# A gated linear attention fused with a cosine-gated MLP: products handed to VectorE in the first five pairs, a fourth load buffer, DMA turns one pair earlier, and a new order of steps

## The chip, the core and the metric

The kernel runs on one core of a Trainium2 chip. Its time is device microseconds of one execution, and the number compared is the median of several executions. Three executions of the kernel before took 182.08, 183.91 and 185.15 us, so the median is 183.91 us and the spread is about 1.7%.

## What is computed

Attention with a forget gate runs over 4 batches and 8 heads, 768 positions of 48 values each. Its output is laid out as 3072 rows of 384 values and goes through two matrices with `h * cos(h)` between them.

```python
f = 1.0 / (1.0 + np.exp(-f_logit))
for t in range(S):
    state = f[:, :, t, :, None] * state + np.einsum('bhd,bhe->bhde', k[:, :, t], v[:, :, t])
    y[:, :, t] = np.einsum('bhd,bhde->bhe', q[:, :, t], state)
h = x @ w_in           # x: 3072 x 384, w_in: 384 x 2048
g = h * np.cos(h)
out = g @ w_out        # w_out: 2048 x 384
```

Inputs and output are float32. Inside the kernel the matrix products run in bfloat16.

## The kernel before

**Tiling.** The 768 positions of a batch are cut into stretches of 256, which the code calls pairs (two chunks of 128, or two positions to each of 128 partitions). There are 12 pairs, three to a batch, and the state of a batch runs through its three pairs. The MLP works on units of tokens: units 0 and 1 are the two halves of pair 0 (128 rows each), and unit m from 2 on is pair m-1 (256 rows).

**Steps of a pair n.** Every step has a name, and the names are used below.

- Loads `f n`, `k n`, `q n`, `v n` bring 384 KB each from device memory (line 296). Pairs 0 and 1 load f, k and q in two halves of four heads, `f0.0` and `f0.1` and so on.
- ScalarE makes the gate: `ex` (exp, L329), `ln` (L333), `fx` (exp again, L347), `fy` (add one, L344).
- `qa` (L338 or L341) multiplies q by a gate, `ka` (L351) multiplies k by a gate, and `ad` (L363) adds two logarithms. `cum` (L374 and L380, TensorE) sums the logarithms over time, and `eb` and `ei` (L391 or L395, ScalarE) take the exponential of the sums.
- `qm` and `km` (L404) multiply q and k by these exponentials and write the tile `qk` in bfloat16. They come in two halves of four heads.
- Turning: in pairs 0 to 4 `tq` and `tk` transpose `qk` on TensorE (L434, sixteen 128x128 transposes a pair), and `qkt` copies the result out of PSUM (L439; the profile shows the copies at their helper's line L197). In pairs 5 to 11 two DMA transposes do it (L423), issued by the SP queue.
- `vb` casts v and `vt` (four of them) places it with zeroes around it (L197).
- `sc` makes the scores (L454, TensorE) and `am` masks them (L458, VectorE). `ps` is the outer product for the state (L476); `st` (L494) and `sz` (L500) carry and decay the state on VectorE. `y` and `yi` (both L528) sum the output, and `xe` copies it to SBUF.

**Steps of a unit m.** `h` is the first product (L576), twelve matmuls of 128 columns or six of 256 for each step; `co` is the cosine on ScalarE (L581); `g` multiplies h by it on VectorE (L558); `o` is the second product (L592, four matmuls of 384 columns each); `ot` copies a row block out, and `out` stores it (L603). The weights come in eight pieces: `w0.x` is a piece of w_in, `w1.x` one of w_out, 768 KB each (L282), cast by `wc` (L197).

**PSUM and fillers.** PSUM has eight banks. `h`, `co`, `g`, `sc` and `am` use two banks at a time, so four such values can be in flight, and an `h` step waits for the `g` or `am` that last used its banks. `zf` steps (L264) are matmuls of zeroes, 51 of them, that stand between TensorE's first real steps.

**Order.** No planner runs when the kernel is built. The string `ORDER` (L36 to L117) lists all steps in one sequence, each with its engine (T TensorE, S ScalarE, V VectorE, G GpSimd, Y SP) and the buffer or bank that its result takes. `emit` (L617) writes them out in that sequence, and each engine then does its own steps strictly in order. A step that may run on more than one engine names them in `G.step(...)`, and the letter in `ORDER` picks one. `SLOTS` (L30) is the number of buffers of each kind. The loads run on the queues of SP and ScalarE, and a load waits for the load eight places ahead of it in the program, besides the users of its buffer.

In the profile VectorE is DVE and GpSimd is POOL.

Of the kernel before, what the change touches and what calls it, by code (L numbers as in the profile page):

```python
# [15 lines left out]
B, H, S, D = 4, 8, 768, 48  # L16
# [20 lines left out]
f0.0:Y0 f0.1:Y zf0:T0 zf1:T2 q0.0:Y2 zf2:T3 zqk.2:G zf3:T4 k0.0:Y1 zf4:T5 zf5:T6 f1.0:Y2 zf6:T7  # L37
zf7:T1 k0.1:Y zf8:T0 zf9:T2 v0:Y1 zf10:T3 zsz.0:V zf11:T4 zsp.0:V f1.1:Y zsz.3:V ex0.0:S zf12:T5
zvt.0:V zf13:T6 zvt.1:V zf14:T7 ln0.0:S0 k1.0:Y2 zf15:T0 fx0.0:S cum0.0:T1 ex0.1:S f3:Y1 zf16:T2
zf17:T3 zf18:T4 ln0.1:S zf19:T5 k1.1:Y ka0.0:V zf20:T6 fx0.1:S cum0.1:T7 q0.1:S zf21:T0 q1.0:Y1  # L40
zf22:T2 zf23:T3 eb0.0:S0 zf24:T4 ei0.0:S1 zf25:T5 v1:Y0 ei0.1:S zf26:T6 km0.0:V2 eb0.1:S zf27:T1
ex1.0:S ka0.1:V zf28:T0 zf29:T7 zvt.2:V zf30:T2 qa0.0:V ln1.0:S0 zf31:T3 q1.1:Y qm0.0:V vb0:G2
fx1.0:S cum1.0:T6 zsp.1:V tk0.0:T0 km0.1:V tq0.0:T ex1.1:S vt0.2:G1 ps0.0:T3,2 ps0.1:T zf32:T4
ln1.1:S zqk.1:G sz0.01:V0 zf33:T5 ei1.0:S2 cum1.1:T7 vt0.0:G eb1.0:S2 qa0.1:V tk0.1:T4 qkt0.0:S3
sz0.00:V zf34:T6 f2:Y0 qm0.1:G zf35:T1 st0.11:V zf36:T3 w0.0:Y1 zf37:T5 sz0.11:V3 fx1.1:S w0.1:Y4
sc0.0:T0 ka1.0:G ei1.1:S st0.10:V tq0.1:T eb1.1:S zf38:T6 sz0.10:V ex3:S zf39:T7 km1.0:G0 qkt0.1:V0
zf40:T3 zf41:T2 am0.0:V2 ln3:S1 yi0:T5 sc0.1:T2 vt0.1:G zf42:T4 zf43:T6 fx3:S ad3:G0 zf44:T7 qa1.0:V
zf45:T4 vt0.3:S zf46:T0 qm1.0:V zf47:T1 zqk.0:V vb1:G1 cum3:T6 ka1.1:V tk1.0:T7 am0.1:V0 eb3:S1
tq1.0:T km1.1:G ps1.0:T0,1 qkt1.0:S3 zf48:T4 zf49:T4 zf50:T4 qa1.1:V ps1.1:T vt1.1:G2 vt1.3:S
sc1.0:T2 zsp.2:V qm1.1:V y0:T7 ex2:S st1.00:V q3:Y1 tq1.1:T4 am1.0:V0 tk1.1:T w0.2:Y3 ei3:S0 ln2:S0  # L50
qkt1.1:V4 wc0.0:G vt1.2:S sz1.00:V0 xe0.1:S0 st1.01:V xe0.0:S sz1.01:V sc1.1:T4 ad2:G2 w0.3:Y1
vt1.0:S yi1:T0,3 am1.1:V2 fx2:S k3:Y2 h0.00:T6 fy3:S w1.0:Y2 wc0.1:G cum2:T2 y1:T ei2:S1 xe1.0:S1
h1.00:T4 xe1.1:V qa3:G eb2:S0 h1.01:T st1.11:V st1.10:V qm3.1:G2 h2.00:T2 sz1.11:V3 sz1.10:V h0.01:T
co1.0:S2 qm3.0:G h2.01:T co0.0:S0 wc0.2:G q2:Y1 g1.0:V4 h2.11:T0 h2.10:T co2.0:S1 g0.0:V0 wc0.3:G
h2.20:T4 co2.1:S2 h2.21:T g2.0:V3 h1.10:T6 ka3:G w1.1:Y1 co2.2:S3 f5:Y2 h1.11:T g2.1:V km3.0:G fy2:S
h0.10:T2 k2:S0 h0.11:T wc1.0:G g2.2:V co1.1:S0 h2.31:T0 co0.1:S1 g1.1:V h2.30:T qa2:G w1.2:Y2
o0.0:T5 v2:Y0 co2.3:S3 zsz.2:V qm2.1:G1 g0.1:V o1.0:T6 o2.0:T4 qm2.0:G wc1.1:S g2.3:V tq3.1:T7
tq3.0:T2 tk3.0:T km3.1:G tq2.0:T3 o0.1:T qkt3.0:V0 w1.3:Y1 ka2:G v3:Y2 o2.1:T f4:Y1 k5:Y1 tk3.1:T
ex5:S km2.0:G sc3.0:T0 q4:Y2 qkt3.1:V4 o1.1:T ln5:S0 am3.0:V2 km2.1:G tk2.0:T tq2.1:T2 o3.1:T7 fx5:S
ad5:G0 qkt2.0:V2 f7:Y0 wc1.2:S tk2.1:T o3.0:T qkt2.1:V3 sc2.0:T0 sc3.1:T2 fy5:S vb2:G0 am2.0:V3  # L60
# [128 lines left out]
def describe(nc, cpool, ppool, q, k, v, f_logit, moe_w_in, moe_w_out, out):  # L189
# [121 lines left out]
    def pair(n):  # L311
# [38 lines left out]
        def lead_k(e, t, w):  # L350
            eng(e).tensor_mul(out=w.ap[:, :, 0, :], in0=w.ap[:, :, 0, :], in1=t.ap[:, :, 0, :])  # L351
# [363 lines left out]
```

## Time and profile before

| what | us |
|---|---|
| median of three executions (182.08 to 185.15) | 183.91 |
| the execution that was profiled | 182.69 |
| its span, first to last instruction | 180.9 |
| TensorE busy | 171.6 (95%) |
| VectorE busy | 140.1 (77%) |
| ScalarE busy | 128.4 (71%) |
| GpSimd busy | 108.8 (60%) |

The profile is of one execution, and times in it run from its first instruction. The execution took 1.8 us more than its span. A busy share is an average over stages: VectorE, ScalarE and GpSimd are all busy for nine tenths of some stretches in the first 100 us, and GpSimd has nothing left after about 131 us. TensorE's busy time holds 49 recorded filler matmuls. Matmuls overlap, so the time from one start to the next is a better price than a duration.

### The profile page before, as it was taken

To read this page: it belongs to the slowest core of one execution; us is meant where nothing else is said; L and a number is where in the kernel's file an instruction comes from. 1 tells how busy PE (TensorE), PEld (TensorE's weight loads), DVE (VectorE), ACT (ScalarE), POOL (GpSimd) and SP (SyncE) were. 2 spreads that over 40 slices of the span, in tenths; PEclk is the share of its full clock that TensorE was granted. 3 is DMA by queue.
4 is the path that set the end of the run, shared out by engine and by line. 5 is a ranking of instruction groups with operands and counts; after the bars stand their busy time and mean duration, and the time that the engine had idled before them with its cause. 6 is when DMAs were issued, how large, how long until landed. Compare 5 with 4: busy or idle time off the path is not lost.

```text
span 180.9 us, 5972 instructions
## 1 busy us (share of the span) xinstructions
PE 171.6 (95%) x2539; PEld 124.7 (69%) x2541; DVE 140.1 (77%) x214; ACT 128.4 (71%) x182; POOL 108.8 (60%) x136
## 2 busy tenths in 40 slices
PE   7999759998999999999999999999999999999991
PEld 2464458875668876788667886668867887866560
DVE  6359977996896999999998899978889986672210
ACT  4578689897779999987999989629951856243110
POOL 3069478998779999999658999999910000000000
PEclk9999999999999999999999999999999999999998
DMA  5999899899999999999999999913963100100233
GB/s 130 258 261 265 302 327 343 191 315 334 283 261 276 279 188 267 257 263 190 240 243 259 300 153 228 140 45 62 148 116 134 43 4 4 43 0 0 91 130 130
DMA packets 72282, 33.94 MB, mean 188 GB/s; under 512 B 65344, under 2 KB 70720, under 8 KB 72256
## 3 DMA queue, kind: packets, MB, share of 16 engines
q1 hardware_dynamic: 69216, 32.28, 74.6%
q10 hardware_dynamic: 3040, 1.28, 2.8%
q8 instruction: 20, 0.33, 0.8%
q14 instruction: 6, 0.05, 0.1%
HBM read 25.17 MB, written 4.72 MB: 165 GB/s over the span
## 4 chain that ended last, share of the span: by engine, by line
PE 50%; POOL 19%; DMA 12%; DVE 5%; SPq 5%; issue 4%; ACT 3%; POOLq 0%; DVEq 0%; ACTq 0%
PE ps L592 20%; PE ps L576 19%; POOL qk L404 10%; DMA q<-in_q_dram 7%; PE ps L264 5%; SPq L296 3%; DMA g<-in_moe_w_out_dram 3%; PE ps L528 3%; DMA f<-in_f_logit_dram 2%; POOL k L351 2%; POOL vt L197 2%; POOL q L341 2%; POOL w_in_bf L197 2%; DVE am L458 1%; PE ps L454 1%
## 5 line engine op out<-in xcount | busy, mean ns | idle before, releaser
L558 DVE TENSOR_TENSOR g<-ps,co 128x1024 bf16<-128x1024 f32 x48 | 60.2, 1308 | 10.9 <-ACT co L581 9.2
L592 PE MATMUL ps<-w_out_bf,g 128*128 128x384 bf16 x384 | 68.3, 326 | 0.0
L576 PE MATMUL ps<-x,w_in_bf 128*128 128x256 bf16 (+1 forms) x624 | 66.7, 264 | 0.4 <-POOL w_in_bf L197 0.4
L581 ACT ACTIVATE co<-ps,halfpi 128x1024 bf16<-128x1024 f32 x48 | 52.3, 1112 | 15.3 <-PE ps L576 14.2
L576 PEld LDWEIGHTS <-w_in_bf 128*128 128x128 bf16 x624 | 56.3, 98 | 8.8 <-POOL w_in_bf L197 0.6
L592 PEld LDWEIGHTS <-g 128*128 128x128 bf16 x384 | 36.0, 98 | 22.1 <-DVE g L558 0.3
L458 DVE TENSOR_TENSOR am<-ps,pmask 128x1024 bf16<-128x1024 f32 x24 | 28.6, 1217 | 2.5 <-PE ps L454 2.3
L404 POOL TENSOR_TENSOR qk<-k,bi 128x384 bf16<-128x384 f32 x22 | 21.8, 1001 | 2.0 <-DVE k L351 1.0
L404 POOL TENSOR_TENSOR qk<-q,b 128x384 bf16<-128x384 f32 x21 | 20.8, 1001 | 1.1 <-DVE q L338 0.5
L197 POOL COPY vt<-vb 64x384 bf16<-64x384 bf16 x36 | 18.1, 505 | 1.5
L197 ACT COPY ot<-ps 128x384 f32<-128x384 f32 (+1 forms) x13 | 5.8, 450 | 16.3 <-PE ps L592 11.1
L500 DVE TENSOR_TENSOR sz<-ps,b 64x192 bf16<-64x192 f32 x40 | 13.9, 354 | 3.1 <-PE ps L476 2.1
L264 PE MATMUL ps<-zero 128*128 128x512 bf16 x49 | 14.1, 434 | 1.5 <-DVE zero L203 1.2
L197 DVE COPY ot<-ps 128x384 f32<-128x384 f32 (+1 forms) x13 | 6.8, 522 | 9.7 <-ACT ot L197 5.2
L197 POOL CAST vb<-v 128x768 bf16<-128x768 f32 x10 | 8.8, 879 | 8.4 <-DMA v<-in_v_dram 7.7
L329 ACT ACTIVATE f<-f 128x768 f32<-128x768 f32 (+1 forms) x14 | 10.5, 750 | 3.6 <-DMA f<-in_f_logit_dram 3.6
L363 POOL TENSOR_TENSOR sp<-ls 128x384 bf16<-128x384 f32 x10 | 10.0, 1000 | 4.5 <-ACT ls L333 4.4
L494 DVE TENSOR_TENSOR ps<-ps,sz 64x192 f32<-64x192 f32 x32 | 11.6, 365 | 1.4 <-PE ps L476 0.5
L341 POOL TENSOR_TENSOR q<-f,q 128x384 f32<-128x384 f32 x10 | 10.0, 1002 | 2.1 <-PE ps L528 1.3
L351 POOL TENSOR_TENSOR k<-k,f 128x384 f32<-128x384 f32 (+1 forms) x11 | 10.6, 962 | 1.0 <-DMA k<-in_k_dram 0.7
L454 PE MATMUL ps<-qkt 48*64 48x128 bf16 x384 | 9.2, 220 | 1.9 <-ACT x L197 1.9
L264 PEld LDWEIGHTS <-zero 128*128 128x128 bf16 x51 | 5.0, 108 | 7.2 <-issue 3.0
(60 smaller groups left out, 162.3 us busy)
## 6 DMA issues: line engine op xcount, KB each, us to landing
v<-in_v_dram SPq DMA_DIRECT2D x12, 384.0 KB, 6.2
out_dram<-ot SPq DMA_DIRECT2D x22, 192.0 KB, 2.8
f<-in_f_logit_dram SPq DMA_DIRECT2D x10, 384.0 KB, 5.9
q<-in_q_dram SPq DMA_DIRECT2D x9, 384.0 KB, 5.5
k<-in_k_dram SPq DMA_DIRECT2D x9, 384.0 KB, 6.0
g<-in_moe_w_in_dram SPq DMA_DIRECT2D x4, 768.0 KB, 7.9
g<-in_moe_w_out_dram SPq DMA_DIRECT2D x4, 768.0 KB, 7.9
f<-in_f_logit_dram SPq DMA_DIRECT2D x4, 192.0 KB, 3.9
```

The costliest lines, as they stand in the source:

```text
L197: (nc.scalar.copy if e == "ACT" else eng(e).tensor_copy)(out=o, in_=i)
L264: G.step(f"zf{i}", ("PE",), lambda e, dump=dump: nc.tensor.matmul(dump.ap, lhsT=zero[:, 0:128], rhs=zero, start=True, stop=True), writes=[ ...
L341: eng(e).tensor_mul(out=w.ap[:, :, 0, :], in0=t.ap[:, :, 1, :], in1=w.ap[:, :, 0, :])
L351: eng(e).tensor_mul(out=w.ap[:, :, 0, :], in0=w.ap[:, :, 0, :], in1=t.ap[:, :, 0, :])
L404: G.step(f"{nm}{n}.{u}", ("POOL", "DVE") if cut else ("POOL",), lambda e, u=u, j=j, src=src, dec=dec: eng(e).tensor_mul(out=qkp[u][j].ap[: ...
L458: G.step(f"am{n}.{u}", ("DVE",), lambda e, u=u, sc=sc: nc.vector.tensor_mul(out=am[u].ap.rearrange("p r b n -> p (r b) n"), in0=sc.ap.rear ...
L494: nc.vector.tensor_add(out=view()[s], in0=view()[s], in1=S0.ap[s, :, r, :])
L500: eng(e).tensor_mul(out=new.ap[s, :, r, :].rearrange("p (u a) n -> p u a n", u=2), in0=view()[s].rearrange("p (u a) n -> p u a n", u=2), i ...
L558: nc.vector.tensor_mul(out=o.rearrange("p b (n e) -> p b e n", e=2), in0=ph.ap.rearrange("p (b e n) -> p b e n", e=2, n=64), in1=co.ap.rea ...
L576: nc.tensor.matmul(ph.ap[:, i * T:(i + 1) * T].rearrange("p (g t) -> p g t", t=C), lhsT=w_in_bf[:, kk, f0:f0 + 128], rhs=xa[:, :, kk, :], ...
L581: G.step(f"co{m}.{j}", ("ACT",), lambda e, ph=ph, co=co: nc.scalar.activation(out=co.ap, in_=ph.ap, func=AF.Sin, bias=halfpi), reads=[ph], ...
L592: nc.tensor.matmul(po.ap[:, 0:DM], lhsT=gT.ap[:, j, i * C:(i + 1) * C], rhs=w_out_bf[:, j, :], start=(po.first and j == 4 * s), stop=(po.f ...
```

## The change

The fixed numbers, and the engines that some steps may use:

```diff
-TURN_QK = range(5, 12)
+TURN_QK = range(4, 12)
+SHARED = range(5)
-SLOTS = {"f": 3, "k": 3, "q": 3, "v": 3, ...
+SLOTS = {"f": 4, "k": 4, "q": 4, "v": 4, ...
-ZEROS = 51
+ZEROS = 65
...
-        cut = n in HALVES
+        cut, either = n in HALVES, ("POOL", "DVE") if n in SHARED else ("POOL",)
...
-            G.step(f"qa{n}{u}", ("DVE",) if cut else ("POOL",), ...
-            G.step(f"ka{n}{u}", ("POOL", "DVE") if cut else ("POOL",), ...
+            G.step(f"qa{n}{u}", ("DVE",) if cut else either, ...
+            G.step(f"ka{n}{u}", either, ...
-            G.step(f"ad{n}", ("POOL",), ...
+            G.step(f"ad{n}", either, ...
-                G.step(f"{nm}{n}.{u}", ("POOL", "DVE") if cut else ("POOL",), ...
+                G.step(f"{nm}{n}.{u}", either, ...
-f0.0:Y0 f0.1:Y zf0:T0 zf1:T2 q0.0:Y2 zf2:T3 zqk.2:G zf3:T4 k0.0:Y1 zf4:T5 zf5:T6 f1.0:Y2 zf6:T7
+f0.0:Y3 v0:S1 zf0:T0 f0.1:S f1.1:Y1 zf1:T1 zsp.0:G k0.0:Y3 q0.0:S1 zsp.1:G zf2:T2 zsz.3:G f1.0:Y
```

The whole `ORDER` string is new. Counted over it, thirteen steps of the kinds `qa`, `km`, `qm` and `ad` go from GpSimd to VectorE: `ad3`, `ad4`, `km1.0`, `km1.1`, `km2.0`, `km3.0`, `km3.1`, `km4.1`, `qa3`, `qm0.1`, `qm2.0`, `qm2.1` and `qm3.1`. Three go the other way (`km0.0`, `qm1.0`, `qm1.1`), so the net is ten. The copies `qkt1.1`, `qkt3.0` and `qkt3.1` go from VectorE to ScalarE. Of the `ot` copies nine go to ScalarE and five to VectorE. Twelve `vt` copies go from GpSimd to ScalarE and six the other way, and the two casts `wc1.1` and `wc1.2` go from ScalarE to GpSimd. The steps `tq4` and `tk4` on TensorE and their two copies are gone; two DMA transposes on SP take their place. Lines of the changed kernel are two higher than before.

The last stores change too: before, the last row block to be finished is copied and stored in two halves (`ot22.0`, `ot22.1`); after, the last is row block 20, copied whole by ScalarE and stored whole by SP.

**The start, ScalarE.** Before, ScalarE begins with its table and the gate of pair 0. In the rows, `f_0_94` is buffer 0 of the gate tile f, `sp` holds logarithms, `b` and `bi` the exponentials.

```order
L634 ACT_TABLE_LOAD
L329 ACTIVATE f_0_94<-f_0_94 128x384
L333 ACTIVATE sp_0_106<-f_0_94 128x2x4x48
L347 ACTIVATE f_0_94<-sp_0_106 128x4x48
L329 ACTIVATE f_0_94<-f_0_94 128x384
L333 ACTIVATE sp_0_106<-f_0_94 128x2x4x48
L347 ACTIVATE f_0_94<-sp_0_106 128x4x48
L296 DMA q_2_102<-in_q_dram 128x4x96
```

After, three loads and the cast of v0 stand ahead of the first logarithm.

```order
L298 DMA v_1_107<-in_v_dram 128x8x96
L298 DMA f_3_97<-in_f_logit_dram 128x4x96
L298 DMA q_1_103<-in_q_dram 128x4x96
L636 ACT_TABLE_LOAD
L331 ACTIVATE f_3_97<-f_3_97 128x384
L199 CAST vb_0_124<-v_1_107 128x768
L335 ACTIVATE sp_1_111<-f_3_97 128x2x4x48
L349 ACTIVATE f_3_97<-sp_1_111 128x4x48
L393 ACTIVATE b_0_115<-ps_3_165 128x196
L393 ACTIVATE bi_0_118<-ps_3_165 128x192
L331 ACTIVATE f_3_97<-f_3_97 128x384
L331 ACTIVATE f_1_95<-f_1_95 128x384
```

The loads `v0`, `f0.1` and `q0.0` moved to ScalarE's queue, `vb0` moved there from GpSimd, and pair 1's gate now begins between the two halves of pair 0's.

**The start, SP.** Before, the second half of k0 (the second row with `k_1_98`) is the sixth load.

```order
L296 DMA f_0_94<-in_f_logit_dram 128x4x96 x2
L296 DMA q_2_102<-in_q_dram 128x4x96
L296 DMA k_1_98<-in_k_dram 128x4x96
L296 DMA f_2_96<-in_f_logit_dram 128x4x96
L296 DMA k_1_98<-in_k_dram 128x4x96
L296 DMA v_1_104<-in_v_dram 128x8x96
```

After, it is the eighth on SP (the second row with `k_3_101`), with three more on ScalarE's queue beside them.

```order
L298 DMA f_3_97<-in_f_logit_dram 128x4x96
L298 DMA f_1_95<-in_f_logit_dram 128x4x96
L298 DMA k_3_101<-in_k_dram 128x4x96
L298 DMA f_1_95<-in_f_logit_dram 128x4x96
L298 DMA q_1_103<-in_q_dram 128x4x96
L298 DMA q_3_105<-in_q_dram 128x4x96
L298 DMA k_0_98<-in_k_dram 128x4x96
L298 DMA k_3_101<-in_k_dram 128x4x96
```

So the load `k0.1` moved from sixth to eleventh in all, and the load `q1.0` ahead of it now waits for `v0`.

**The first MLP units, VectorE.** Before, from the first `g` of units 1, 0 and 2 on, eight of these products (`ps` times `co`) run with one memset among them.

```order
L558 TENSOR_TENSOR g_4_147<-ps_2_160,co_2_150 128x8x2x64
L558 TENSOR_TENSOR g_0_143<-ps_3_161,co_0_148 128x8x2x64
L558 TENSOR_TENSOR g_3_146<-ps_1_159,co_1_149 128x8x2x64
L558 TENSOR_TENSOR g_3_146<-ps_0_158,co_2_150 128x8x2x64
L558 TENSOR_TENSOR g_3_146<-ps_2_160,co_3_151 128x8x2x64
L558 TENSOR_TENSOR g_4_147<-ps_3_161,co_0_148 128x8x2x64
L231 MEMSET sz_2_137 128x192
L558 TENSOR_TENSOR g_0_143<-ps_1_159,co_1_149 128x8x2x64
L558 TENSOR_TENSOR g_3_146<-ps_0_158,co_3_151 128x8x2x64
```

After, from the fourth of them on, products of pair 3 stand between them.

```order
L560 TENSOR_TENSOR g_4_151<-ps_2_164,co_1_153 128x8x2x64
L406 TENSOR_TENSOR qk_0_121<-k_2_100,bi_2_120 128x8x48
L560 TENSOR_TENSOR g_2_149<-ps_1_163,co_2_154 128x8x2x64
L560 TENSOR_TENSOR g_4_151<-ps_3_165,co_1_153 128x8x2x64
L343 TENSOR_TENSOR q_1_103<-f_2_96,q_1_103 128x8x48
L406 TENSOR_TENSOR qk_0_121<-k_2_100,bi_2_120 128x8x48
L406 TENSOR_TENSOR qk_0_121<-q_1_103,b_0_115 128x8x48
L560 TENSOR_TENSOR g_3_150<-ps_0_162,co_3_155 128x8x2x64
L560 TENSOR_TENSOR g_4_151<-ps_2_164,co_2_154 128x8x2x64
```

`km3.0`, `qa3`, `km3.1` and `qm3.1` came in from GpSimd, and each has both its inputs in SBUF, while `g` has one in PSUM.

169 lines of the change are left out of this document (85 added, 84 removed).

## The prediction

> **What bounds the kernel now.** I read the page's busy shares first, then TensorE's timeline, the idle times in it, and last the chain of waits.
>
> ```profile
> PE 171.6 (95%) x2539; PEld 124.7 (69%) x2541; DVE 140.1 (77%) x214; ACT 128.4 (71%) x182; POOL 108.8 (60%) x136
> DMA  5999899899999999999999999913963100100233
> 24.29 0.42 PE L454 MATMUL ps<-qkt 48*64 48x128 bf16 x16 [1.89 <-ACT x L197]
> 24.84 0.52 PE L528 MATMUL ps<-qkt,sz 128*32 128x128 bf16 x24
> 25.29 0.84 PE L576 MATMUL ps<-x,w_in_bf 128*128 128x128 bf16 x12
> 25.97 0.33 PE L374 MATMUL ps<-sp,incl 128*128 128x384 bf16 x1
> 26.31 0.63 PE L528 MATMUL ps<-am,vt 128*32 128x128 bf16 x32
> 32.03 5.47 PE L576 MATMUL ps<-x,w_in_bf 128*128 128x256 bf16 x72 [0.36 <-POOL w_in_bf L197]
> 43.63 0.62 PE L434 MATMUL ps<-ident,qk 128*128 128x128 bf16 x8 [0.54 <-POOL qk L404]
> 164.22 13.02 PE ps L592 x80
> ```
>
> TensorE is the bound from about 25 us on. In brackets stands its idle time ahead of a row: after 25.29 us, where the first MLP product starts, it idles 0.36 and 0.54 us and has no other gap above 0.1 us until its last matmul ends at 177.2. The last row, from the chain of waits, is dense too: 80 matmuls of 384 columns in 13.02 us, 163 ns each. So a change can gain in three places only: an earlier start of the dense part, less TensorE work in it, a shorter tail. It can lose wherever another engine comes late. The DMA engines are full from the second slice to the 26th of 40, and the other engines feed TensorE with small margins.
>
> **The sum, part by part.** It is made against the profiled execution, 182.69 us, which lies 1.2 us under the median of 183.91; the difference goes onto the median.
>
> *Pair 4 by DMA.* Sixteen transposes leave TensorE.
>
> ```profile
> 65.95 1.06 PE L434 MATMUL ps<-ident,qk 128*128 128x128 bf16 x16
> 66.84 0.81 PE L592 MATMUL ps<-w_out_bf,g 128*128 128x384 bf16 x4
> qkt<-qk SPq DMA_TRANSPOSE x14, 4.1
> ```
>
> From start to next start that is 0.89 us of a dense stage, so **-0.9**. The two DMA turns take 4.1 us each, but by the new order some 18 `h` and `o` steps of 0.65 us (11.8 us) stand between pair 3's last `y` and pair 4's first score, so they are covered; without that cover each would cost up to 4.1. SP waits for `km4.0` before it issues them; `f6` and `v5` queue behind and are not needed for 10 us.
>
> *The start.* Compare the moment of the first `h` step. Before it is 25.29, with `yi1` (0.45) done and `cum2` (0.34) not; after, it is the other way round, so the equal point is 25.29 - 0.45 + 0.34 = 25.2.
>
> ```profile
> 0.00:7.00 7.00, 5.81 (x18) 2.26 (x19) 2.94 (x20) 3.99 (x7) 1.61 (x9) 1.00 0.69 169
> 7.00:12.00 5.00, 5.00 (x75) 2.99 (x72) 2.87 (x8) 2.93 (x8) 1.95 (x3) 1.00 1.23 272
> 0.73 1.28 ACT L634 ACT_TABLE_LOAD   x1 [0.73 <-PEq L699]
> 4.09 0.52 ACT L333 ACTIVATE sp<-f 128x384 bf16<-128x384 f32 x1
> 4.64 0.36 ACT L347 ACTIVATE f<-sp 128x192 f32<-128x192 bf16 x1
> 8.68 0.33 ACT L391 ACTIVATE bi<-ps 128x192 f32<-128x192 f32 x1 [0.79 <-PE ps L380]
> 3.98 1.56 SPq L296 DMA_DIRECT2D v<-in_v_dram  x1
> 9.98 1.23 POOL L197 CAST vb<-v 128x768 bf16<-128x768 f32 x1 [7.70 <-DMA v<-in_v_dram]
> 12.25 0.36 DVE L500 TENSOR_TENSOR sz<-ps,b 64x192 bf16<-64x192 f32 x1 [1.71 <-PE ps L476]
> ```
>
> The last column of the first two rows is GB/s: 1.18 MB are in by 7 us, then 0.272 MB a microsecond. The load `k0.1` was the sixth; now ten are ahead of it, and its last byte is number 2.36 million, moved at 7 + 1.18/0.272 = 11.3 us. It lands about 1.3 us later, near 12.7. ScalarE comes as late. Its three loads take some 2 us (v's issue 1.56 at most), then its table 1.28, so it begins near 4.1; v0, alone at the head of its queue, should land near 6 (it took 6.0 from issue behind six others), and the cast waits for that about 1.3; a wait for `cum0.0` is some 0.4. Up to `fx1.1`, which `ka1.1` needs, stand four `ex` and four `ln` (0.52), one cast (0.83), four `fx` (0.36) and three exponentials (0.33): 7.4 us, so 13.2. From there VectorE has two `ka` (0.36), `km0.1` and `qm0.1` (0.53) ahead of the first `sz`: 14.8 us instead of 12.25.
>
> ```profile
> L458 DVE TENSOR_TENSOR am<-ps,pmask 128x1024 bf16<-128x1024 f32 x5 | 6.1, 1215 | 0.2 <-PE ps L528 0.2
> L197 DVE COPY qkt<-ps 128x1024 bf16<-128x1024 bf16 x6 | 4.1, 686 | 1.8 <-PE ps L434 1.8
> L500 DVE TENSOR_TENSOR sz<-ps,b 64x192 bf16<-64x192 f32 x8 | 2.8, 354 | 1.9 <-PE ps L476 1.7
> L494 DVE TENSOR_TENSOR ps<-ps,sz 64x192 f32<-64x192 f32 x6 | 2.2, 366 | 0.2
> 12.25:45.85 33.60, 29.31 (x487) 21.85 (x491) 29.11 (x43) 28.96 (x42) 27.83 (x28) 1.00 1.03 296
> ```
>
> From there to `xe0.1`, which `h1.00` needs, the new order has on VectorE 4 `sz` (0.36), 2 `st` (0.37), 2 `qa` (0.35), 2 memsets (0.27), 4 `am` (1.21), 2 `km` and `ad3` (0.53, taken for all products of 384), one `qkt` (0.69) and `xe` itself (0.56): 11.2 us. So `h1.00` starts near 26.0, **+0.8**. The bounds: the 65 fillers (16 take 5.9 us as now, 49 go at 0.22) and the 6.8 us of real work let it start at 24.4 at the earliest (-0.8); if v0 lands as late as its present 9.98, near 29 (+3.8). I take the middle sum, since each step of it has a row. The 14 added fillers lie in waits and cost nothing while those last; without that cover they are 14 x 0.22 = 3.0, inside the upper bound.
>
> *The first MLP units and pairs 2 and 3.* The two present gaps go (-0.36 - 0.54 = **-0.9**): `wc0.2` no longer stands behind `qa3` and `qm3.1` on GpSimd, nor the second turn behind a GpSimd product. What is late next is VectorE. The last row above is its stretch up to the copy `qkt2.1`: 29.11 us busy of 33.60. To the same copy the new order has one `am` more, three `qkt` less and nine products and sums more, net, at 0.53 in place of some slower ones (below): about 2.4 us more work in a stretch that has 4.5 us idle. On the whole it fits. In place it doesn't: `qkt2.0` and `qkt2.1` now stand behind `am3.1`, three products, `am3.0` and `ad4`, and I find `sc2.0` and `sc2.1` waiting about **+0.9** together (bounds 0, and 2.4, all the work added).
>
> *Products on VectorE beside GpSimd.* These are the rows that price a VectorE operation with both inputs in SBUF.
>
> ```profile
> 12.64 0.36 DVE L338 SCALAR_TENSOR_TENSOR q<-f,q 128x192 f32<-128x192 f32 x1
> 16.62 1.10 DVE L338 SCALAR_TENSOR_TENSOR q<-f,q 128x192 f32<-128x192 f32 x1
> 17.76 1.06 DVE L404 TENSOR_TENSOR qk<-q,b 128x384 bf16<-128x384 f32 x1
> 20.80 0.67 DVE L404 TENSOR_TENSOR qk<-q,b 128x384 bf16<-128x384 f32 x1
> 10.04 0.49 DVE L404 TENSOR_TENSOR qk<-k,bi 128x384 bf16<-128x384 f32 x1
> 16.51 1.00 POOL L363 TENSOR_TENSOR sp<-ls 128x384 bf16<-128x384 f32 x1
> 17.45 0.95 POOL L197 CAST vb<-v 128x768 bf16<-128x768 f32 x1
> 20.44 0.62 POOL L197 COPY vt<-vb 64x384 bf16<-64x384 bf16 x1
> ```
>
> Beside a running GpSimd operation the same form takes 1.10 in place of 0.36, and 1.06 and 0.67 in place of about 0.53; two others (10.04, 12.64) paid nothing. Over these five the extra is (0.75 + 0.53 + 0.14)/5 = 0.28 us. Eleven moved operations lie before `qkt2.1`, and GpSimd is busy 27.83 of 33.60 us there (0.83): 11 x 0.83 x 0.28 = 2.6, of which I let 0.9 fall into the margins of about half a microsecond that `h1.11` and `o3.0` have to their banks: **+1.7** (bounds 0 and 4.6, the rival below). `km4.1` and `ad4` come later beside slack.
>
> *Loads and buffers.* With four buffers a load may be issued earlier, but the DMA row is full until slice 26 and no load stops TensorE after 25 us: 0. The other moves (`vt`, `vb`, `ot`, `qkt`, `wc`) add about 5 us to ScalarE (128.4 busy) and take some 10 from GpSimd: 0 while both have idle time at these places; by the order none is due within a microsecond.
>
> *Tail.*
>
> ```profile
> out_dram<-ot SPq DMA_DIRECT2D x22, 192.0 KB, 2.8
> out_dram<-ot SPq DMA_DIRECT2D x1, 96.0 KB, 1.6
> 177.26 0.32 ACT L197 COPY ot<-ps 128x192 f32<-128x192 f32 x1 [1.27 <-PE ps L592]
> 177.61 0.36 DVE L197 COPY ot<-ps 128x192 f32<-128x192 f32 x1 [2.69 <-ACT ot L197]
> 175.51 0.48 ACT L197 COPY ot<-ps 128x384 f32<-128x384 f32 x1 [0.98 <-PE ps L592]
> ```
>
> Two half copies in a row (0.71) become one whole (0.48), and a store of 96 KB one of 192: -0.2 to +1.0 us. The 2.8 is a median among other traffic, so I take **+0.3**.
>
> Sum: -0.9 + 0.8 - 0.9 + 0.9 + 1.7 + 0.3 = +1.9 us. The profiled execution would take 184.6, the median 185.8 us, 1% more.
>
> **Rivals.** *Slower by more than 2%: each product waits out GpSimd.* Place: VectorE from 15 to 47 us. If a product that meets a GpSimd operation always waits for its end, and the operations last 1.0 us, the wait is half of one on average: 11 x 0.83 x 0.5 = 4.6 and nothing falls into margins of half a microsecond; the median would be 183.9 + 0.2 + 4.6 = 188.7. For it: the two long products end 0.2 and 0.4 us after the GpSimd operation that they began beside, which is most of their own length. Against it: the cheap rows. It decides from 3.5 us, that is 0.32 us for each of the eleven. [...]
>
> *Faster, within 2%: VectorE keeps up.* If the start comes at its bound (-0.8), the gaps go (-0.9), no score waits, GpSimd takes the delays itself, pair 4 gains 0.9 and the tail 0.2, the sum is -2.8 and the median 181.1. For it: 4.5 us of idle time on VectorE. Against: `k0.1` and v0 must land earlier than the rates allow. More cannot be gained, for the rest is dense TensorE work that stays.
>
> *The change does nothing:* the loads are bound by DMA, the fillers by `w0.0`, and the ends cancel: 183.9. The first forecast holds this in its range.
>
> **The numbers.** About 2% (3.7 us) is what a measurement of this kernel can tell from no change. The forecast, 0 to +3.7 with 185.8 as likeliest, has 0.45; VectorE keeping up, no change included, 0.20, with 0.04 of it beyond 2% by the scatter of runs; waiting out GpSimd 0.30; a late load or a later start of both, up to 191, 0.05. So faster 0.04, same 0.61, slower 0.35. The range from 182.0 to 190.0 leaves out about 1 in 10 on either side; the likeliest case alone is 183.9 to 187.6.
>
> **What would show it.** First `h` step (L578 after) near 26.0 us: 24.4 to 25 speaks for the faster rival, past 27 for a late v0 or k0.1. [...] TensorE idle at L456 near 47 us about 0.9; no gap above 0.5 after 60 us; 64 transposes left. A gap in the second half, or a wait on a DMA turn at pair 4's scores, would prove the sum wrong.

## The result and the profile after

The changed kernel takes 190.03 us (median of four, 189.89 to 190.28); the kernel before took 183.0 beside it (182.03 to 185.15). The ratio is 1.0405 (95% interval 1.0328 to 1.0482): 4% slower, where 1% was forecast, and just past the upper end of the range. Medians are over all executions, while a ratio leaves out those that lie more than 1.5% above the fastest of their kernel (the 185.15 here), so it is not quite the quotient of two medians.

The profiled execution after took 190.28 us with a span of 188.5; before it was 182.69 and 180.9. TensorE's timeline of the changed kernel shows where the first 60 us went. Columns: start, duration, engine, line, operation, tiles, shape, count, and in brackets the idle time ahead of the row and what ended it.

```profile
26.48 1.50 PE L578 MATMUL ps<-x,w_in_bf 128*128 128x128 bf16 x24
27.92 0.52 PE L530 MATMUL ps<-qkt,sz 128*32 128x128 bf16 x24
29.65 0.63 PE L530 MATMUL ps<-am,vt 128*32 128x128 bf16 x32 [1.21 <-issue]
...
42.42 0.40 PE L436 MATMUL ps<-ident,qk 128*128 128x128 bf16 x4 [0.42 <-DVE qk L406]
...
43.65 0.38 PE L436 MATMUL ps<-ident,qk 128*128 128x128 bf16 x4 [0.18 <-DVE g L560]
...
50.08 0.84 PE L436 MATMUL ps<-ident,qk 128*128 128x128 bf16 x12 [1.01 <-DVE qk L406]
...
52.27 0.42 PE L456 MATMUL ps<-qkt 48*64 48x128 bf16 x16 [0.48 <-DVE qkt L199]
53.78 0.42 PE L456 MATMUL ps<-qkt 48*64 48x128 bf16 x16 [1.08 <-DVE qkt L199]
54.13 4.46 PE L594 MATMUL ps<-w_out_bf,g 128*128 128x384 bf16 x16
58.51 0.69 PE L478 MATMUL ps<-vb,qk 64*64 64x48 bf16 x48
```

Four things are to be seen. The first `h` step starts at 26.48. Between two rows of the sums `yi1` and `y1` TensorE stands still for 1.21 us, and the profile names nobody ("issue"). From 42 to 54 us it waits five times for VectorE, 3.17 us in all. And the sixteen 384-column matmuls at 54.13 take 274 ns each from one start to the next, (58.51 - 54.13)/16, where such a matmul took 163 in the dense part. The granted clock says why. The columns of this table are the stretch, its length, the busy time (and count) of TensorE, weight loads, VectorE, ScalarE and GpSimd, then the granted clock, the DMA share and GB/s.

```profile
48.00:50.00 2.00, 1.06 (x20) 0.45 (x17) 2.00 (x3) 1.95 (x4) 1.61 (x1) 1.00 1.10 251
50.00:52.00 2.00, 1.72 (x20) 1.29 (x20) 2.00 (x4) 1.95 (x3) 1.06 (x2) 1.00 1.18 281
52.00:54.00 2.00, 0.64 (x32) 0.48 (x32) 1.72 (x3) 1.93 (x5) 1.89 (x3) 1.00 1.24 265
54.00:56.00 2.00, 2.00 (x25) 1.00 (x14) 1.75 (x2) 0.76 (x2) 1.90 (x4) 0.71 0.94 201
56.00:58.00 2.00, 2.00 (x8) 0.99 (x7) 1.07 (x2) 0.48 (x1) 0.09 (x1) 0.50 0.04 9
```

TensorE is busy 3.4 of the 6 us from 48 to 54, and after that its clock is 0.50. The trace has it at half for 3.41 us, from 54.86 on, and half of that is 1.7 us. It fits the matmuls: sixteen at 111 ns extra are 1.8 us.

The waits come from VectorE's products. These rows of its timeline are `km1.0`, `km3.0`, `qm3.1`, `km2.0` and `qm2.0`:

```profile
20.35 1.17 DVE L406 TENSOR_TENSOR qk<-k,bi 128x384 bf16<-128x384 f32 x1
37.11 0.54 DVE L406 TENSOR_TENSOR qk<-k,bi 128x384 bf16<-128x384 f32 x1
41.01 1.36 DVE L406 TENSOR_TENSOR qk<-q,b 128x384 bf16<-128x384 f32 x1
47.10 1.19 DVE L406 TENSOR_TENSOR qk<-k,bi 128x384 bf16<-128x384 f32 x1
48.21 1.81 DVE L406 TENSOR_TENSOR qk<-q,b 128x384 bf16<-128x384 f32 x1
```

And this is what GpSimd does beside four of them (beside `km3.0`, at 37.11, it does nothing):

```profile
19.96 1.15 POOL L199 CAST vb<-v 128x768 bf16<-128x768 f32 x1
40.71 1.25 POOL L406 TENSOR_TENSOR qk<-q,b 128x384 bf16<-128x384 f32 x1 [3.59 <-DVE q L343]
46.87 1.00 POOL L406 TENSOR_TENSOR qk<-k,bi 128x384 bf16<-128x384 f32 x1
47.80 1.80 POOL L199 CAST w_out_bf<-g 128x1536 bf16<-128x1536 f32 x1
```

Add start and duration. GpSimd ends at 21.11, 41.96, 47.87 and 49.60; the products that began beside it end at 21.52, 42.37, 48.29 and 50.02. Each ends 0.41 to 0.42 us after GpSimd's instruction, so it has waited for that instruction and then done its work. Alone, `km3.0` takes 0.54. The price of these four products is therefore not an average: it is what GpSimd's instruction still has to run when the product begins, plus 0.41 us. `qm2.0` meets a cast of 1536 columns just begun, which has 1.39 us to go, and takes 1.81.

### The profile page after: what moved, and what is told of

It is laid out like the page before. It is cut to its first block, busy times and chain, and to the rows that moved or that the text cites. A ratio compares the mean times of both kernels' runs of the same rounds, so it can differ in the third digit from the quotient of the medians.

```text
span 188.5 us, 5947 instructions
## 1 busy us (share of the span) xinstructions
PE 177.9 (94%) x2535; PEld 125.9 (67%) x2539; DVE 143.5 (76%) x211; ACT 132.6 (70%) x193; POOL 102.0 (54%) x126
## 4 chain that ended last, share of the span: by engine, by line
PE 66%; DVE 18%; ACT 4%; issue 4%; POOL 3%; DMA 2%; SPq 1%; DVEq 0%; ACTq 0%
PE ps L578 25%; PE ps L594 23%; PE ps L266 7%; DVE g L560 5%; PE ps L530 4%; DVE qk L406 3%; PE ps L456 3%; DVE am L460 3%; DMA out_dram<-ot 2%; DVE sz L502 2%; PE ps L478 2%; POOL qk L406 2%; DVE ps L496 1%; DVE qkt L199 1%; PE ps L376 1%
## 5 line engine op out<-in xcount | busy, mean ns | idle before, releaser
L594 PE MATMUL ps<-w_out_bf,g 128*128 128x384 bf16 x384 | 69.8, 332 | 0.0
L406 POOL TENSOR_TENSOR qk<-q,b 128x384 bf16<-128x384 f32 x19 | 19.4, 1031 | 14.9 <-DVE q L340 5.9
L199 ACT COPY ot<-ps 128x384 f32<-128x384 f32 (+1 forms) x17 | 7.4, 442 | 20.2 <-PE ps L594 15.8
L406 POOL TENSOR_TENSOR qk<-k,bi 128x384 bf16<-128x384 f32 x17 | 16.9, 1001 | 5.6 <-ACT bi L397 3.6
L266 PE MATMUL ps<-zero 128*128 128x512 bf16 x61 | 18.2, 436 | 1.5 <-DVE zero L205 1.2
L199 POOL COPY vt<-vb 64x384 bf16<-64x384 bf16 x30 | 15.3, 509 | 6.3 <-ACT vb L199 4.1
L266 PEld LDWEIGHTS <-zero 128*128 128x128 bf16 x65 | 6.3, 108 | 8.5 <-issue 3.8
L365 POOL TENSOR_TENSOR sp<-ls 128x384 bf16<-128x384 f32 x8 | 8.3, 1040 | 6.3 <-ACT ls L335 6.2
L456 PEld LDWEIGHTS <-qkt 48*64 48x64 bf16 x384 | 6.3, 106 | 6.4 <-DVE qkt L199 2.9
L199 DVE COPY ot<-ps 128x384 f32<-128x384 f32 x9 | 4.9, 549 | 7.4 <-PE ps L594 7.4
```

What stands on the lines that cost most here:

```text
L199: (nc.scalar.copy if e == "ACT" else eng(e).tensor_copy)(out=o, in_=i)
L266: G.step(f"zf{i}", ("PE",), lambda e, dump=dump: nc.tensor.matmul(dump.ap, lhsT=zero[:, 0:128], rhs=zero, start=True, stop=True), writes=[ ...
L406: G.step(f"{nm}{n}.{u}", either, lambda e, u=u, j=j, src=src, dec=dec: eng(e).tensor_mul(out=qkp[u][j].ap[:, :, :, 0:D], in0=swap(src.ap), ...
L456: nc.tensor.matmul(o[t, r, 2 * a + g, :].rearrange("p (e n) -> p e n", e=2), lhsT=qkv(u)[s, 1, a, g, x, :], rhs=qkv(u)[s, 0, a, g, :, :], ...
L594: nc.tensor.matmul(po.ap[:, 0:DM], lhsT=gT.ap[:, j, i * C:(i + 1) * C], rhs=w_out_bf[:, j, :], start=(po.first and j == 4 * s), stop=(po.f ...
```

## Experiments

Theory: products wait out GpSimd, `qm2.0` worst of all; the waits this gives TensorE halve its clock as well; the rest is a later start. Rivals: the products are long for reasons of their own; the clock halves for other reasons; the start is bound by VectorE, or by loads. The kernel before, run beside each group, had medians of 182.91 to 183.33, so a difference of 0.4 us between two rows of this table is not safe.

| kernel | median us (lowest to highest) | ratio to before (95%) |
|---|---|---|
| changed | 190.03 (189.89 to 190.28) | 1.0405 (1.0328 to 1.0482) |
| cast later | 188.56 (186.61 to 189.08) | 1.0275 (1.0198 to 1.0352) |
| cast and `ad4` later | 186.70 (186.60 to 186.86) | 1.0194 (1.0140 to 1.0248) |
| fillers, first try | 191.47 (190.16 to 191.93) | 1.0462 (1.0392 to 1.0532) |
| fillers, free banks | 187.87 (187.66 to 188.62) | 1.0296 (1.0240 to 1.0351) |
| products back | 187.13 (187.06 to 187.20) | 1.0249 (1.0189 to 1.0310) |
| `xe0.1` on ScalarE | 186.76 (186.57 to 187.20) | 1.0231 (1.0179 to 1.0283) |
| eight fillers fewer | 186.34 (185.81 to 187.40) | 1.0210 (1.0133 to 1.0287) |
| 28 fillers fewer | 186.97 (185.99 to 187.28) | 1.0216 (1.0154 to 1.0279) |
| cast on ScalarE | 186.44 (186.38 to 186.66) | 1.0199 (1.0143 to 1.0254) |
| before, pair 4 by DMA | 186.57 (185.03 to 188.57) | 1.0158 (1.0080 to 1.0235) |
| the same, no bank waits | 187.02 (185.37 to 188.66) | 1.0212 (1.0122 to 1.0302) |
| before, two products | 183.20 (181.71 to 184.87) | 0.9999 (0.9953 to 1.0044) |

### The cast out of the way

```diff
-wc1.3:G   (on GpSimd between km2.1 and ad5)
+wc1.3:G   (on GpSimd behind ad5)
```

> The changed kernel with one step moved: the cast wc1.3 goes on GpSimd from ahead of qm2.0 and qm2.1 to behind ad5, so that GpSimd is idle while VectorE takes these two products. Theory that a product on VectorE waits out the GpSimd instruction beside it: qm2.0 falls from 1.81 to about 0.55 us, tq2.0's wait of 1.0 us on TensorE goes, and the two later waits shrink by 0.3 together: 190.0 - 1.3 = 188.7; if the clock then holds too, 186.8. Rival, that qm2.0 is long for a reason of its own (its operands, VectorE's own queue): qm2.0 stays at 1.8 and the time at 190.0.

Measured: 188.56. VectorE's rows of `km2.0`, and of `qm2.0` and `qm2.1` together:

```profile
46.94 1.18 DVE L406 TENSOR_TENSOR qk<-k,bi 128x384 bf16<-128x384 f32 x1
48.04 1.01 DVE L406 TENSOR_TENSOR qk<-q,b 128x384 bf16<-128x384 f32 x2
```

`qm2.0` and `qm2.1` take 1.01 us for both, where they took 2.28; `km2.0`, which still meets `km2.1`, stays at 1.18. Nothing but GpSimd's neighbouring instruction was changed, so the theory holds and the rival falls. TensorE's waits in that place are now these; the 1.01 at the first turn is gone, and the last row is new, `o2.3` waiting for the cast that was moved:

```profile
50.84 0.42 PE L456 MATMUL ps<-qkt 48*64 48x128 bf16 x16 [0.39 <-DVE qkt L199]
51.91 0.42 PE L456 MATMUL ps<-qkt 48*64 48x128 bf16 x16 [0.65 <-DVE qkt L199]
...
53.56 2.11 PE L594 MATMUL ps<-w_out_bf,g 128*128 128x384 bf16 x12 [0.48 <-POOL w_out_bf L199]
```

The four executions are a second experiment. One took 186.61 us at a mean granted clock of 1.000; three took 188.37, 188.74 and 189.08 at 0.990, 0.991 and 0.989. A stretch of 3.41 us at half clock in a span of 187 is a mean of 0.991. So the same program either loses its clock once or doesn't, and one execution against three makes that worth about 2.1 us. That a mean of 0.99 stands for one such stretch is read from other traces: the four kept traces with a mean of 0.990 or 0.991 hold exactly one stretch of 3.41 us ahead of the program's end, and the nine with 0.997 or more hold none. Of this kernel only the whole-clock execution was traced.

### `ad4` out of the way too

```diff
-ad4:V   (on VectorE between qkt2.0 and qkt2.1)
+ad4:V   (on VectorE behind am2.0)
```

> The same as the kernel with the cast moved, and ad4 on VectorE moved from between the copies qkt2.0 and qkt2.1 to behind the mask am2.0. If VectorE's lateness is what TensorE waits for, the wait of sc2.1 (1.1 us) shrinks by ad4's 0.98 as well, all waits between 49 and 54 us together are under 1 us, the clock stays whole and the kernel takes 190.0 - 1.3 - 0.9 - 1.9 = 185.9. If the clock halves in spite of it, 187.8. If neither move matters because TensorE waits for something else there, 190.0.

Measured: 186.70, and 186.60 to 186.86 in four executions, all at a clock of 1.000. TensorE's three waits are now 1.20 us in all:

```profile
50.39 0.42 PE L456 MATMUL ps<-qkt 48*64 48x128 bf16 x16 [0.39 <-DVE qkt L199]
50.99 0.42 PE L456 MATMUL ps<-qkt 48*64 48x128 bf16 x16 [0.18 <-DVE qkt L199]
...
52.79 2.11 PE L594 MATMUL ps<-w_out_bf,g 128*128 128x384 bf16 x12 [0.63 <-POOL w_out_bf L199]
```

I expected 185.9: 0.6 of the difference is the cast's new wait. Two steps of the order, with no work removed, are worth 3.3 us of the 7.0 that the change cost.

### Fillers in the waits

```diff
 qm2.1:V am3.0:V2 km2.1:G ln4:S0
+zf65:T4 zf66:T5 zf67:T4
 tq2.0:T1
```

(and so ahead of `sc2.0` in bank 1 and of `sc2.1` in bank 1)

> The changed kernel with nine more matmuls of zeroes in TensorE's three waits between 49 and 54 us (three ahead of tq2.0, two ahead of sc2.0, four ahead of sc2.1, 0.22 us each); nothing else moves. Clock theory: these waits are what halves TensorE's clock near 54.9 us, so with the fillers the sixteen matmuls that took 279 ns each take 163 again, and the kernel gains up to 1.9 us: 188.2 in place of 190.0. Rival: the halved clock comes from something else (the table, the temperature, the other engines), the fillers change nothing or cost what of them sticks out of the waits: 190.0 to 190.5.

Measured: 191.47, slower. The edit was at fault: banks 4 and 5 still held the scores that `am3.0` was to mask, so the first filler waited for that mask.

```profile
51.43 0.81 PE L267 MATMUL ps<-zero 128*128 128x512 bf16 x3 [2.59 <-DVE am L461]
```

It tells only that a filler needs a bank that nobody will read; with this wait in it two of the four executions were at a clock of 0.991 and two at 1.000. The second try takes such banks:

```diff
 qm2.1:V am3.0:V2 km2.1:G ln4:S0
+zf65:T0 zf66:T0 zf67:T0 zf68:T0
 tq2.0:T1
```

> The changed kernel with ten more matmuls of zeroes in its three waits between 49 and 54 us, now in banks that nobody holds there (bank 0 ahead of tq2.0, bank 4 ahead of sc2.0, bank 1 ahead of sc2.1); the products and casts stay where the change put them. Clock theory: the stretch of 3.41 us at half clock goes in all executions and the time falls from 190.0 by some 1.9 to 188.1, the mean granted clock from 0.99 to 1.00. Rival: the waits don't matter for the clock, the time stays at 190.0 and the clock at 0.99.

Measured: 187.87, four executions between 187.66 and 188.62, all at a clock of 0.997 or above; the changed kernel's four were at 0.988 to 0.990. The same stretches as above:

```profile
48.00:50.00 2.00, 1.86 (x17) 0.95 (x15) 2.00 (x3) 1.97 (x4) 1.07 (x1) 1.00 1.21 268
...
52.00:54.00 2.00, 1.88 (x35) 0.84 (x24) 1.48 (x3) 1.94 (x5) 1.85 (x4) 1.00 1.14 255
54.00:56.00 2.00, 2.00 (x14) 1.21 (x13) 2.00 (x3) 0.50 (x2) 1.52 (x3) 1.00 0.71 159
```

The sixteen matmuls from the scores to the next row take 2.70 us (56.30 - 53.60), where they took 4.38, though VectorE's two products are as long as before (2.28 us). Line numbers are one higher in the kernels with added fillers:

```profile
53.60 2.77 PE L595 MATMUL ps<-w_out_bf,g 128*128 128x384 bf16 x16
56.30 0.69 PE L479 MATMUL ps<-vb,qk 64*64 64x48 bf16 x48
```

Ten matmuls that compute nothing make the kernel 2.2 us faster. In the two profiles 1.7 of it lies in these sixteen matmuls, as the clock theory says, and 0.5 was there at 43 us already, ahead of the first of the ten. The theory holds.

What decides can be read from the traces in part. In all fourteen, every stretch of whole or half clock except the last, which the end cuts off, is a whole multiple of 3.413 us (47.79 in the changed kernel is 14 of them, 174.08 in the kernel before is 51, 13.65 in the one with 28 fillers fewer is 4), and the first begins between 3.9 and 7.1 us after the span's start: at 4.3 with the cast moved and at 7.1 in the changed kernel, whose first 45 us are the same program. Cut each trace into windows of that length, counted from its first stretch: in the five windows ahead of a drop, the one at the end of the program left aside, TensorE was idle for 1.57 to 2.12 of the 3.41 us (1.57 here), and no whole-clock window with less than 1.5 us of idle time was followed by one. Four windows with 1.56 to 1.96 us idle (one of them in the kernel before, 1.61 us idle from 22.81 to 26.22) were not followed by one either, so idle time alone doesn't decide. Where the windows fall settles which waits share one, and the two starts, 4.3 and 7.1 us with the same program up to the waits, put them at different places. That this is why three executions of one program lose the clock and one doesn't is an estimate and was not shown.

### Pair 2's products back on GpSimd

```diff
-km2.0:V2 qm2.0:V qm2.1:V am3.0:V2 km2.1:G
+km2.0:G2 qm2.0:G am3.0:V2 km2.1:G qm2.1:G
```

(on top of the kernel with the cast and `ad4` moved)

> The kernel with the cast wc1.3 and ad4 moved, and besides the products km2.0, qm2.0 and qm2.1 back on GpSimd. If handing pair 2's products to VectorE gains nothing there, the time is the same as without this edit, 186.7, within 0.5: GpSimd needs 4 x 1.0 us for the four products from 46.8 and is done at 50.8, where VectorE and GpSimd together are done at 48.6, but VectorE then has its masks and copies 1.6 us earlier. If the shared products are worth their place, the second turn waits for qm2.1 and o2.3 for the cast: 188 to 189.

Measured: 187.13 against 186.70. The waits only change owners: the second turn waits for GpSimd, `sc2.1` for the copy behind it.

```profile
49.22 0.40 PE L436 MATMUL ps<-ident,qk 128*128 128x128 bf16 x4 [0.32 <-POOL qk L406]
...
51.42 0.42 PE L456 MATMUL ps<-qkt 48*64 48x128 bf16 x16 [0.51 <-DVE qkt L199]
```

So handing over these three products is worth 0.4 us at best, when the cast stands elsewhere. What they cost with the cast where the change put it was not run by itself; moving the cast and `ad4` away from them brought 3.3.

### The start

Three kernels on top of the one with the cast and `ad4` moved. First the copy `xe0.1`, which the first `h` step needs, leaves VectorE:

```diff
-xe0.1:V   (on VectorE behind am1.1 and am1.0)
+xe0.1:S   (on ScalarE behind xe0.0)
```

> The kernel with the cast wc1.3 and ad4 moved, and besides the copy xe0.1, which h1.00 needs, taken from VectorE to ScalarE. Theory that the start is late because VectorE is full from 12 to 26 us, with its products stretched by GpSimd: the first h step starts 0.4 to 0.6 us earlier (26.1 to 25.6) and the end too: 186.7 - 0.5 = 186.2. Rival, that the start is late because TensorE's own steps and fillers end late: the first h step stays at 26.1 and the time at 186.7.

Measured: 186.76, no change, so VectorE alone does not bound the first `h` step: my theory fell in that form. TensorE's rows, fillers (L266) ahead of the first `h`:

```profile
25.16 1.04 PE L266 MATMUL ps<-zero 128*128 128x512 bf16 x4
26.03 1.50 PE L578 MATMUL ps<-x,w_in_bf 128*128 128x128 bf16 x24
```

In the changed kernel this copy does end just ahead of the step, which starts at 26.48:

```profile
25.83 0.55 DVE L199 CAST x<-ps 128x384 bf16<-128x384 f32 x1
```

So both end together there, VectorE's chain and TensorE's own row. TensorE had hardly a gap from 12 to 27 us. That is because it was doing fillers, so the next kernel leaves out the last eight:

```diff
-zf57 ... zf64
-ZEROS = 65
+ZEROS = 57
```

> The kernel with the cast, ad4 and xe0.1 moved, and without the last eight fillers (zf57 to zf64; 57 are left). Theory that the start is now set by TensorE's own row of steps, with fillers in it that no longer lie in waits: the first h step starts 0.9 to 1.4 us earlier (26.0 to some 24.9) and the end by as much, 186.8 to about 185.7, less what y1 then waits for the mask am1.0. Rival, my prediction's assumption that added fillers lie in waits: the first h step stays near 26.0, a wait stands where the fillers were, and the time is 186.8.

Measured: first `h` at 25.15, as early as the equal point of the kernel before (25.2), but the time only 0.4 lower, 186.34 (one of the four executions, 187.40, at a clock of 0.991).

```profile
25.15 1.50 PE L578 MATMUL ps<-x,w_in_bf 128*128 128x128 bf16 x24 [0.53 <-DVE am L460]
...
26.93 0.28 PE L530 MATMUL ps<-am,vt 128*32 128x128 bf16 x8
28.87 0.52 PE L530 MATMUL ps<-am,vt 128*32 128x128 bf16 x24 [1.66 <-issue]
```

The stand-still without a named cause has grown to 1.66 us and stands eight matmuls later, in the middle of `y1`. Eight fillers are sixteen instructions of TensorE (a weight load and a matmul each), and so are eight matmuls of `y1`. In both kernels TensorE stops at the same place in its list of instructions, about the 704th, although the steps there differ: it is the start of `y1` in one and its middle in the other. The trace has a transfer of instructions (16 KB) around that stop in both: from 27.1 to 28.2 us in the changed kernel, which goes on at 29.65, and from 26.4 to 27.5 here, going on at 28.87. That TensorE has run out of instructions fits all of this, but it is argued and not shown; no run removed that transfer. The profiles of two other kernels (`xe0.1` on ScalarE, cast on ScalarE) put the stop down to GpSimd's cast of `w_in` instead; in the kernel with eight fillers fewer no GpSimd instruction ends between 27.3 and 28.9 us, so it isn't that one there.

The third leaves out all fillers from `zf37` on:

> The same without all fillers from zf37 on (37 are left, 28 gone, 6 us of TensorE time). Fillers in the path: 185.7 or below, with the waits of the start now visible and named. Fillers that keep the clock: TensorE does 12 us of start with long waits in it, the granted clock halves for 3.41 us there, and 1.7 us or more of the gain is lost again: 186.5 to 188.

Measured: 186.97, the same within the scatter, with another mixture. The stretches:

```profile
12.00:17.00 5.00, 3.27 (x67) 2.14 (x64) 4.40 (x14) 3.38 (x9) 0.02 (x1) 0.99 1.30 266
17.00:22.00 5.00, 2.85 (x33) 2.07 (x34) 5.00 (x6) 4.16 (x7) 5.00 (x5) 0.50 1.04 374
22.00:30.50 8.50, 8.38 (x198) 6.97 (x196) 5.47 (x11) 6.90 (x12) 8.24 (x9) 0.50 1.08 361
```

Without fillers the clock is at half from 16.9 to 30.5 us, so that the first `h` starts at 26.27 again, and the unnamed stand-still is gone. That TensorE at half speed doesn't get ahead of whatever it waited for would explain this, but was not tested. What 28 fillers cost they give back as clock.

### The cast on ScalarE

```diff
-wc1.3:G   (on GpSimd behind ad5)
+wc1.3:S   (on ScalarE behind ln4)
```

> The kernel with the cast, ad4 and xe0.1 moved, but the cast wc1.3 on ScalarE behind ln4 in place of GpSimd behind ad5. The step o2.3 then doesn't wait for the cast any more (0.63 us): 186.8 - 0.6 = 186.2, if ScalarE's 1.5 us more there delay nothing; 186.8 if the copies of vt2 or the gate of pair 5 come late for it.

Measured: 186.44 against 186.76, all four executions under the other's median, though the two ran at different times and 0.3 us is within what the kernel before moved. The wait of `o2.3` is gone; half of the gain returns as a wait of 0.29 us at 56.7 us, where the sums of pairs 2 and 3 begin.

### Parts of the change in the old order

```diff
-TURN_QK = range(5, 12)
+TURN_QK = range(4, 12)
-km4.0:G ... tq5.0:Y0 km4.1:G ... tq4.1:T4 tk4.1:T ... qkt4.0:V1
+km4.0:G tq4.0:Y1 ... km4.1:G tq4.1:Y3 tq5.0:Y0
```

> The kernel before with one part of the change alone: pair 4 is turned by DMA (tq4.0 and tq4.1 on the SP queue ahead of tq5.0, as soon as km4.0 and km4.1 are done), its sixteen transposes and two copies gone; the scores sc4.1 and sc4.0 go behind the four o steps that followed them, so that the DMA turns have 3 to 5 us. My term of the sum: 183.0 - 0.9 = 182.1. Rival: two more transfers of 4 us on a full DMA hold back the loads of pair 6 or the turns of pair 5, and nothing is gained: 183 or above.

Measured: 186.57, not 182.1. TensorE's longest waits in it:

```profile
PE ps L374 <- DVE am L458: 2.2, 1, 2.2
PE ps L454 <- ACT x L197: 1.7, 1, 1.7
...
PE ps L454 <- DMA qkt<-qk: 0.7, 1, 0.7
```

The first is of my making: I gave `cum6` a bank that `am4.0` still reads. The second the kernel before has too (1.9 us). The third is a score that waits for a DMA turn of a later pair, at 92.8 us, as the rival said; the kernel before has no such wait. Another try with the banks in order:

> The kernel before with pair 4 turned by DMA, as in the first try of it, but with the scores sc4.1 and sc4.0 one after the other in the same two banks and cum6 in its old bank, so that no step waits for a bank. My term of the sum: 183.0 - 0.9 = 182.1. Rival: the two more DMA turns delay other transfers (the turns of pair 5, the loads of pairs 6 and 7) by as much as TensorE gains: 183.0 or above.

Measured: 187.02, the ratio 1.0212. Neither try came under 185 in any execution, so 0.9 us of work taken off TensorE is not to be had in the old order by moving two turns. My term fell there. The profiled execution of the second try, the slowest of the four (188.66), has a score of pair 5 waiting 2.3 us for its DMA turn, at 78.3 us, which the kernel before hasn't: the rival's delay. How much of it the three faster executions had stays open.

The last kernel hands over two products in the old order:

```diff
-qm2.1:G1 ... qm2.0:G
+qm2.1:V1 ... qm2.0:V
```

> The kernel before with one part of the change alone: the products qm2.0 and qm2.1 on VectorE, at their old places in the order. If a VectorE product waits out the GpSimd instruction beside it, they stand beside qa2 and km3.1 (1.0 us each) and take some 1.0 to 1.4 us each in place of 0.55, and the gates g0.1 and g2.3 behind them come up to 2.5 us later, which TensorE feels at o0.1 and after: 183.3 + 0.5 to 1.5. If they only add 0.55 us each, VectorE has room (24.5 of 29.7 us) and the time is 183.3 or 0.5 less, since GpSimd is done earlier.

Measured: 183.20, ratio 0.9999 (0.9953 to 1.0044). I expected 0.5 to 1.5 us more, and missed since the products met nobody. VectorE's rows, and GpSimd's next:

```profile
37.48 0.50 DVE L404 TENSOR_TENSOR qk<-q,b 128x384 bf16<-128x384 f32 x1
...
39.09 0.55 DVE L404 TENSOR_TENSOR qk<-q,b 128x384 bf16<-128x384 f32 x1
```

```profile
39.49 1.00 POOL L351 TENSOR_TENSOR k<-k,f 128x384 f32<-128x384 f32 x1 [2.54 <-DMA k<-in_k_dram]
```

GpSimd waits 2.54 us for the load of k2 while VectorE takes them, 0.50 and 0.55 each. So the same two products cost nothing here and 2.28 us in the changed kernel. No version tried is faster than the kernel before; this one equals it.

## Why the prediction was wrong

The sum from the two profiled executions: 7.6 us. Of it 1.3 is the start (26.48 against the equal point 25.2); -0.9 the two old gaps; 3.2 the five waits for VectorE; 1.7 the clock; 1.2 the stand-still before `y1`; 0.7 all that follows the first `h4` step; -0.5 the end behind the last matmul. The remaining 0.9 lies before that step and was not taken apart.

The forecast was +1.9, so it was 5.7 us short. Its mechanism failed in two steps. The extra of 0.28 us for a product beside GpSimd was an average over five rows, where each product waits out GpSimd's instruction. And a wait on TensorE was counted at its own length, with nothing for what it does to the clock. The size of the miss has more parts: the clock 1.7, pair 4 and the dense part 1.6, the stand-still 1.2, VectorE's waits 0.6, the start 0.5, less 0.8 for the tail, and the 0.9 that was not taken apart.

- **Pair 4 by DMA, -0.9.** The transposes are gone and no score waits for a turn, but the time did not come. From the first `h4` step to the last matmul's end the changed kernel needs 123.1 us (62.20 to 185.27), the kernel before 122.4 (54.84 to 177.22). After and before:

```profile
62.20 4.00 PE L578 MATMUL ps<-x,w_in_bf 128*128 128x256 bf16 x35
...
173.41 11.86 PE L594 MATMUL ps<-w_out_bf,g 128*128 128x384 bf16 x72
```

```profile
54.84 9.33 PE L576 MATMUL ps<-x,w_in_bf 128*128 128x256 bf16 x84
...
169.74 7.48 PE L592 MATMUL ps<-w_out_bf,g 128*128 128x384 bf16 x45
```

  That is 0.7 more, where 0.9 less was forecast. 0.54 of it is one wait at 105 us (for the exponential `bi`, L397), so "none is due within a microsecond" failed, and with it the 0 for "the other moves"; other idle time in this part adds 0.2. Where the other 0.9 went stays open.
- **Start, +0.8, measured +1.3.** The size was about right, in part by luck. "The 14 added fillers lie in waits and cost nothing" failed: taking the copy off VectorE brought nothing as long as they stood there, and leaving out eight as well brought the first `h` to 25.15. No run left them out with the copy still on VectorE. The steps of the forecast's chain add up to 15.0 at the first `sz` (14.30 in the trace) and to 26.1 at the end, not to 14.8 and 26.0; `xe0.1` ended at 26.38.
- **Old gaps, -0.9.** Right; both are gone.
- **VectorE late (+0.9) and the products beside GpSimd (+1.7).** Together 2.6, measured 3.2, at the places named (`sc2.0`, `sc2.1`) and at the turns of pairs 2 and 3. The mechanism is the rival's: each product waits out GpSimd. Twelve moved operations stand ahead of `qkt2.1`, for `ad4`, which the prediction's eleven leave out, is one of them. They took 0.91 us on average (0.49 to 1.81), 0.36 over their own 0.55, past the 0.32 from which that rival was to decide. Its price was 4.6; twelve times 0.36 is 4.3. The rows that I had show it, the cheap ones too: the product at 20.80 ends 0.41 us after the copy that began at 20.44, and the one at 12.64, of half the length, ends 0.21 after this copy of the kernel before:

```profile
12.29 0.50 POOL L197 COPY vt<-vb 64x384 bf16<-64x384 bf16 x1
```

  They were cheap since little of the copy was left to run. The last cheap one, at 10.04, met a cast that is recorded as begun 0.06 us earlier and that took 1.23 us (such casts take 0.88 on average), so there GpSimd was the one that waited. Averaging the five rows hid that the other four end 0.21 to 0.42 us behind GpSimd's instruction; the eight of the changed kernel end 0.41 to 0.42 behind it.
- **What no term held.** The clock, 1.7, and the stand-still, 1.2. Here the waits of 3.2 us brought 1.7 more on the clock; moving the cast and `ad4` took 1.5 us of the waits away, and the time fell by 3.3. Between the medians the clock counts for somewhat less, because by its mean clock (0.987 to 0.991) the kernel before lost it too in 15 of its 27 executions beside the experiments, with a median of 183.33 us against 182.75 in the other twelve. Where it lost it was not traced. In the kernel before with two products it was from 24.41 to 27.82 us, in the fastest of its ten executions, so a lost stretch did not cost the same everywhere: 0.6 us between these medians, 2.1 in the kernel with the cast moved. That its place decides this is an estimate.
- **Loads and buffers, 0.** No wait on a load in the changed kernel's first 60 us is TensorE's. Three buffers in the new order were not tried.
- **Tail, +0.3, measured -0.5.** From the last matmul's end to the end of the span it is 3.2 us, before 3.7.

Of the rivals, "each product waits out GpSimd" (188.7) came nearest, and its mechanism is what the runs show; the clock and the stand-still are in no rival.

## What to carry to other kernels

Before a product with both inputs in SBUF goes to VectorE, look at what GpSimd runs at that moment: price it at the rest of GpSimd's instruction plus a fixed time (0.41 us for 384 columns here), and keep long casts away from it. Price a cluster of waits on TensorE at more than their sum, since the clock may halve behind them (here behind 1.57 us idle out of 3.41, which cost 1.7 us more); filling the waits with matmuls of zeroes, in banks that nobody reads any more, is a cheap test of that. And a filler that stands in a wait costs nothing only as long as the wait is there (here the first `h` came 0.9 us earlier, 25.15 in place of 26.03, without eight of them): after a reorder, count them again.

## What was not expected of the hardware

- In the changed kernel all eight products that begin on VectorE beside a GpSimd product or cast end 0.41 to 0.42 us after it (four are shown above); GpSimd's own instruction is stretched likewise when it comes second (a cast of 1.46 us took 1.80, a product of 1.00 took 1.25).
- TensorE's clock halved for 3.41 us after three waits of 0.5 to 1.1 us with work between them. One execution was traced; by the mean clock (0.988 to 0.991) it was so in all four executions of the changed kernel and in three of four of the kernel with the cast moved. In the kernel with 28 fillers fewer it stayed at half for 13.65 us, four times 3.413.
- TensorE stood still for 0.9 to 1.7 us at about the same instruction of its list in nine kernels, one of which has other steps there. The cause is open.
